# Two split units share one step of exponentials in a fused attention and FFN kernel, with a new order of all work

## The chip, the cores and the metric

The kernel runs on one core of one Trainium2 chip. The metric is the device time of one execution in microseconds; less is better. The core's engines are TensorE (PE; its weight loads are listed as PEld), VectorE (DVE), ScalarE (ACT), GpSimd (POOL) and SyncE (SP), which here issues all DMAs. Each engine works through its own queue in order, and they wait for each other by semaphores.

## The reference

Random-feature attention for 8 batches of 8 heads (576 positions, 64 values a head, 128 features), and an FFN with an exact Gelu over the 4608 resulting rows (512 to 2048 to 512). All is fp32. Cut to what matters:

```python
def phi(x):
    proj = np.einsum('bhsd,md->bhsm', x, omega)
    h = proj - np.sum(x * x, axis=-1, keepdims=True) / 2.0
    h = h - np.max(h, axis=-1, keepdims=True)
    return np.exp(h) / np.sqrt(m)
q_p, k_p = (phi(q_s), phi(k_s))
kv = np.einsum('bhsm,bhsd->bhmd', k_p, v)
z = np.sum(k_p, axis=2)
num = np.einsum('bhsm,bhmd->bhsd', q_p, kv)
den = np.einsum('bhsm,bhm->bhs', q_p, z)[..., None] + 1e-06
attn = (num / den).astype(np.float32)
...
x = np.ascontiguousarray(attn.transpose(0, 2, 1, 3)).reshape(B * S, H * D)
h = x @ w_in
g = 0.5 * h * (1.0 + erf(h * inv_sqrt2))
return (g @ w_out).astype(np.float32)
```

## The kernel before

**Units.** Two heads of one batch are a unit, numbered u = 0 to 31, four to a batch (lines 625 to 640). Units 0 to 7 are computed plainly in fp32 at the start, beside the loading and splitting of the FFN weights. Units 8 to 31 are the split units: fp32 values are taken apart into high and low parts, so that TensorE multiplies narrower numbers and adds the partial products.

**A split unit** runs in three pieces. `split_pre` (line 1069): the transposed k and q come in by DMA, ACT makes the high part (`x_high`, 877, helper line 879), GpSimd the low part (`x_low`, 888); TensorE projects (`proj`, line 896, nine tiles for k; `proj_q`, line 918, four pieces for q); ACT and DVE add the parts and take the maxima; a chain of short steps on ACT and DVE ends in the shifts (`k_shift`, line 914, on GpSimd; `q_shift`, on GpSimd or DVE). `exps_op` (line 1111): one step of ACT, `exps` (line 690), takes exp of the whole buffer, 128x2304, k's half and q's. `split_post` (line 1114): GpSimd rounds exp(k) to fp16 (`k_high`, through the helper line 418), DVE, or GpSimd in the units named by the mask `kl`, makes the low part (`k_low`, line 989); TensorE multiplies with v (`kv_split`, line 1000) and, after a transposition back on DVE and another splitting (`q_back`, `q_high`, `q_low`), makes numerator and denominator (`num`, line 758); ACT and DVE divide (`den` 769, `rcp`, `div` 807), and the result lies in SBUF as the FFN's input.

**The step of exponentials.** ACT holds one table of functions at a time. Exp and Gelu need different ones, and the FFN needs Gelu all along. So `exps` ends, for split units, with a Gelu of one element (line 694) that brings the Gelu table back:

```python
def exps(*us):
    for u in us:
        nc.scalar.activation(u.et, u.et, AF.Exp, bias=kln if u.split else 0.0)
    if us[0].split:
        nc.scalar.activation(wmax[0:1, 1, 0:1], wmax[0:1, 1, 0:1], AF.Gelu)
```

The page shows the two table loads as ACT_TABLE_LOAD of lines 692 and 694.

**Buffers.** The exp buffer exists twice: `et` and `et2` (in the trace `et` and `w`, since `et2` lies in the space of the old weights). `u.eb` (line 634) says which one a unit has: among the split units the second one for even u from 10 on, the first one for the others. So neighbours in the order 10, 11, 12, ... alternate.

**The FFN** runs in 13 blocks of 256 or 384 rows. Block 0 is plain (lines 1182 and 1208), blocks 1 to 3 are split into three partial products (1187; 1211 to 1213), and blocks 4 to 12 form the first matrix product by a scheme of Strassen's kind with seven products (`w_prod`, line 1400, twelve matmuls each), then ACT's Gelu (1425) and high part (1431), DVE's low part (1434), and the second product (`w_mm2`, lines 1498 to 1500: gh x woh, gl x woh, gh x wol). PSUM has eight banks: three for the output sums, two and three for the FFN's first product, its Gelu and the attention.

**The order.** Every piece of work is an `op` with an engine and its dependences, numbered as the program makes it. The string `ORDER` (from line 34) lists all 4950 numbers; `Planner.run` (line 294) emits them in this sequence, letters choosing PSUM banks, and `put` (line 1593) ties each instruction to the one before it on its engine. So each engine's queue is in the string's order. The units are made by the loop around line 1572, which already has a branch for `X['pair']`:

```python
us = [u]
...
    if X['pair'] and u.eb == 1:
        us.append(units[done_u + 1])
    for y in us:
        split_pre(y)
    exps_op(us)
    for y in us:
        split_post(y)
done_u += len(us)
```

Of the kernel before, what the change touches and what calls it, by code (L numbers as in the profile page):

```python
# [28 lines left out]
X = dict(plain=8, kvp=8, eb0=8, ttr=1, pair=0, amax=63, qm=1, xm=0, km=0, prelu=1, n0=4, vs=5,  # L29
# [5 lines left out]
1 2a 3 6 0 7 4 9hda 10 42 11 14f 41 15 12 16 13 44eca 49a 17fh 50 47 51 48 8 22ga 18 45 19 20 43 76 21 46 52bf 23 151 152 157  # L35
77 27ga 55 24 28 53 79ada 56 112 54 31g 154 29c 153 158 57ea 160 62ha 66b 84f 32 58 30 85 111 67 33gc 159 80 82 63 155 86 34
64b 65 35 5 87fh 161 36 114eba 163 81 25 78 115 169 88 83 164 37ca 166 113 59 90 119d 650 92ga 38 165 39 116 40 60 89 91 170
120 68ac 117 93 69 172 167 121 97fa 70 101g 71 175 122dh 171 649 173 123 118 156 685 181 72ae 73 125 126 127ca 74 176 75 177
26 178 652baa 687 102 99e 128 657c 162 651 655 653 98 100 179 187 124 103fg 656 658 104 654 659 132ea 182 136c 183 133 168
105 184 185 106 134h 660ba 663 61 94 107df 108 661 137 664 662 686 95 135 665 129 188 109 138ge 671aa 110 190 139 140 141 193  # L40
666ca 672 667 189 722 688aba 174 96 142hg 292a 191 195 194 675c 199 130 689 196 293 192 180 690 691 294 131 197 296b 146 186
297 198 298 673a 668 295 299 248 669 205 300a 150 721 676 692 674 200 301 147 302 202 249b 306b 201 143 250 203 307 303 251
308 144 677ca 145 252 253 206 693b 207 211 678 256 208 276 679 254 312a 313 304c 680 694 305a 310 695 209 314 757 309 270
318b 212 319 217 213 257 255 148 262 264 425 311 272 316 696ba 214 699 282 697 315 320 317 324a 700 218 698 149 215 322 219
220 321 681ba 204 325 701 326 323 328 329 223 283 682 221 222 683 702ca 224 684 258 225 284 703 330b 707ba 226 327 708 216
# [12 lines left out]
803 1016 555 560a 561 1072 556 1018 390 451 562 789cb 450 1019 559 446 557 447 568b 1077 802 569 1073 1020 1021 965 570 1068
1066 563 566 453 564 790 1022 567 448 565 1078 1023 805 967 791 968 571 1024 574 572 454 575 1025 455 792 582 804 1028 576a
573 577 578 1030 452 969 584b 1032 1051 585 1029 579 586 1031 583 587 590 580 1036 1034 1033 1069ba 1037 1070 1082 1074c 456  # L60
581 1075 591 1079a 1035 970 592a 457 1083 593 1087 1092 1071 1088 971 598 1080 972 588 594 458 1084b 1076 595 1089c 1054 589
599 1085 1093 600b 1156 1096 1081 1097 596 1100 459 601 466 1086 1094aa 597 602 973 1026 1095 1098b 606 608a 1104 1090 609
1052 1101 1099 462 1091 1105 603 1027 1158 607 604 1055 610 1102a 1106b 1038caa 605 1103 1039 611 612 464 1040 1108 1163 1053
1168 614 616b 1041 1107 1159 617 613 1042 618 615 1164 1169 460 1117 1160aa 1109 1165b 1161 1166 1173 1043 624a 465 619 1178
1174 1110 625 806 626 1162 807 461 622 1044 620 1179 1111 1167 1170a 1157 627 1183 621 1045 623 630 632b 1171 467 1112 463
633 628 1172 1113 1184 1175c 1180b 1046 1187 1185aa 634 388 629 1176 1181 635 1047 1191 468 1114 1056 631 638 469 470 1177
391 1195 636 1192 639 1182 1115 1188 637 809a 473 640 1186 477 478 641 810 471 1189b 808 1193c 811 1116 472 479 1196 474 1194
1121 812 1190 1119 1247 815b 1127 1249 816 817 1197a 1048 813 475 1120 1142 1250 1198 1123 1057bc 814 476 1200 1125 642 645
1201 821a 1251aa 1058 1254 1049 643 822 818 827a 480 823 1126 828c 1059 1259 819 1264 1202 1255 1060 1061cb 481 482 1128 1248
820 646 1203 1260 830b 1122 1252 831 1118 1124 1699 483 1062 1063 824 1253 825 832 829b 1701 1064 1145 484 1204 836 833 488  # L70
1129aaa 1130 837 490 1199 1256c 826 1261b 489 834 1143 1269 644 1131 1132 1133 838 1257 1270 835 839a 840 486 1274 1258 485
1262 841 1265 1134 1275 1263 1208 1135 1146 1266b 1271c 491 1278 1267 1136 845 1144 1205 1279 846 1272 1268 1206 487 1276aa
1280b 1282 1700 1137 848b 842 1283 1713 1281 1277 1286 849 1287 850 492 847 1273 854 843 1207 1138 844 1284b 855 1210 493
857a 1050 1285 1147 1212 1288b 1148ca 1149 858 856 1289 1291 1715 1214 859 863 1703 1209 864 1211 1150 1714 1151 1292 494
1716 865 1720 851 852 860 1717ba 1216 853 1725 1233 1152ca 495 1718 1719 800 861 872 1730 1290 1293 862 866b 1217 1139 1294
867 496 868 497 1213 1153 1140 1295 1215 869 873 875a 1296 1220baa 870 1218 1297 1236 1221 874 1222 881 1298 1223 499 876
1726 1721 1219 871 1224 1141 882 1154 1225 877 1303 1155 884b 885 1731 1722c 1727a 498 883 878 1735 1702 1305 1723 1307 1740
890 1309 1705 891 886 1736 1226 1227 879 1728 1741 1306 1704 892 1724 1729 1228 880 1310 1230 1229 1732b 1299 1742aa 1737c
500 1301 1733 1308 893a 1231 1734 894 899 1304 1738 1744 1302 1300 900 887 888 1748 895 1234 1739 1749 1311baa 1312 1313 1314
1315 889 902b 1745 1750c 1743 1746a 1237 1752 1235 1316 901 2249 1317 908 1318 896 897 903 1706 1747 1804 1751 898 1321 1753  # L80
1232 1505 1806 904 905 1238 1322 1811 501 909 1754a 1816 1755 906 503 1324 1817 1239cb 1240 911a 1323 1807 910 1338 1339 912
1340 917 907 913 1808aa 1241 918 919 1506 1341 1242 1342 914 1812 920b 921 1821 1809 1707 915 916 1243bc 1810 1756 1813a 1327
1708 926 1244 922 929a 1805 1822 1325 930 931 1319 1757 1245 923 502 1246 924 1343 1328 1814 925 927 928 1815 935 1758 1818c
1823b 1709 1344 1826 1831 1819 1326 1346 1820 936 1320 1348 932 937 944 938b 1330ac 1824 1759 1329 933 1347 1507 1827 945
1710 939 1835 1711 1760 1331 1832 946 504 1825 940 1828b 1508 941 1349 1712 1532 934 1332 1333 947 1829 948 1839 1761 1350
647 949 1354a 1830 942 1351 1352 1762 1334ba 943 1353 1833ca 1335 1504 1509 950 951 1895 1834 1843 1355 1836 952 1356 953
1360b 1512 1763 1522 1357 1358 1765 1510 1361 1336 1362 1337 954 1359 956 1363 1511 1366a 1844 1840 1847 1845c 1837b 957
# [225 lines left out]
def favor_attention_ffn(ctx: ExitStack, tc: tile.TileContext, qT, kT, v, omT, w_in, w_out, out):  # L313
# [1319 lines left out]
```

## Time and profile before

| | |
|---|---|
| time of three runs, us | 948.91, 952.14, 952.36 (median 952.14) |
| the profiled execution, us | 955.2, its span 953.2 |
| matmuls (instructions on PE) | 7292 |
| busy, us: PE, PEld, DVE, ACT, POOL | 935.6, 669.0, 754.3, 770.6, 480.9 |
| table loads of line 692 and of line 694 | 27 and 24, 1283 ns each |
| Exp of a split unit (line 692) | 24, 2217 ns each |
| mean granted TensorE clock | 0.993 |
| moved by DMA | 71.11 MB, mean 75 GB/s |

A record of a matmul runs from its start to the end of its last result, and neighbours overlap, so PE's busy time is the union of the records. A view by windows gives busy time and count of instructions of each engine in a stretch, then the granted clock, the share of DMA and the rate. In a list by time, the columns are start, duration, engine, line, operation, what it writes and reads, and the count of merged instructions; a bracket names the idle time of the engine ahead of it and who ended it.

### The profile page before, as it was taken

The numbers are of one execution on the slowest core, as the hardware profiler recorded it, in microseconds if no ns is written. First come the engines' busy times: TensorE is split into PE (matmuls) and PEld (weight loads), VectorE is DVE, ScalarE is ACT, GpSimd is POOL, SyncE is SP. The second block draws the span as 40 slices with busy tenths as digits, with TensorE's granted clock in tenths as the row PEclk, the third lists the DMA queues.
The fourth block names the chain that finished last, engine by engine and source line by source line (L and its number), as shares of the span: only waits on it lengthen the run. The fifth ranks groups of instructions, "written<-read, shape, count | busy, mean of one in ns | idle before, by whom it ended". The sixth has DMA issues, their size and how long they took to land.

```text
span 953.2 us, 20399 instructions
## 1 busy us (share of the span) xinstructions
PE 935.6 (98%) x7292; PEld 669.0 (70%) x7292; DVE 754.3 (79%) x2021; ACT 770.6 (81%) x1662; POOL 480.9 (50%) x682
## 2 busy tenths in 40 slices
PE   8999999999999999999999999999999999999998
PEld 7666666666556667777767777777777777777776
DVE  3878999999988899899999899889978775652231
ACT  6988788999789889998899999989688865754453
POOL 1455427788677856575567764863374503140000
PEclk8989999999999999999999999999999999999999
DMA  9864323332322213222212322312112000000000
GB/s 272 242 231 161 114 64 92 87 87 67 75 73 75 66 36 102 64 65 72 76 50 68 87 76 74 89 51 61 39 52 84 2 1 23 2 23 24 1 35 23
DMA packets 46293, 71.11 MB, mean 75 GB/s; under 512 B 13680, under 2 KB 22256, under 8 KB 46192
## 3 DMA queue, kind: packets, MB, share of 16 engines
q1 hardware_dynamic: 46192, 69.81, 25.5%
q8 instruction: 58, 0.95, 0.5%
q14 instruction: 43, 0.35, 0.1%
HBM read 60.36 MB, written 9.44 MB: 73 GB/s over the span
## 4 chain that ended last, share of the span: by engine, by line
PE 57%; ACT 14%; DVE 5%; issue 2%; POOL 1%; DMA 1%; ACTq 0%; DVEq 0%; POOLq 0%
PE p L1400 19%; PE p L1498 7%; PE p L1499 7%; PE p L1500 7%; PE p L1187 5%; PE p L758 2%; PE p L896 2%; PE p L1212 2%; PE p L1211 2%; PE p L1213 2%; PE p L918 2%; PE p L1000 2%; ACT r L879 1%; ACT dt L769 1%; ACT L694 1%
## 5 line engine op out<-in xcount | busy, mean ns | idle before, releaser
L888 POOL TENSOR_TENSOR r<-xt,r 64x256 fp32r<-64x256 f32 (+2 forms) x216 | 168.3, 789 | 166.1 <-ACT r L879 118.9
L1498 PE MATMUL p<-woh,gh 128*128 128x512 f16 (+1 forms) x432 | 161.1, 373 | 0.2 <-ACT o L1220 0.2
L1499 PE MATMUL p<-woh,gl 128*128 128x512 f16 (+1 forms) x432 | 160.3, 371 | 0.4 <-DVE gl L1434 0.4
L1500 PE MATMUL p<-wol,gh 128*128 128x512 f16 (+1 forms) x432 | 160.3, 371 | 0.0
L1400 PEld LDWEIGHTS <-w 128*128 128x128 f16 x1728 | 139.5, 98 | 19.1 <-issue 0.3
L1400 PE MATMUL p<-xh,w 128*128 128x192 f16 (+1 forms) x1152 | 148.2, 243 | 0.0
L1400 PE MATMUL p<-xl,w 128*128 128x192 f16 (+1 forms) x576 | 137.3, 243 | 0.0
L1400 PE MATMUL p<-xh,wih 128*128 128x192 f16 (+1 forms) x432 | 103.3, 243 | 0.0
L1400 PE MATMUL p<-xl,wih 128*128 128x192 f16 (+1 forms) x432 | 103.1, 243 | 0.0
L1400 PE MATMUL p<-xh,wil 128*128 128x192 f16 (+1 forms) x432 | 103.1, 243 | 0.0
L879 ACT CAST r<-xt 128x256 fp32r<-128x256 f32 (+2 forms) x216 | 85.2, 406 | 9.1 <-PE p L896 4.2
L1425 ACT ACTIVATE p<-p,bs 128x384 f32<-128x384 f32 (+1 forms) x108 | 57.9, 539 | 34.6 <-PE p L1400 34.1
L1400 PEld LDWEIGHTS <-wih 128*128 128x128 f16 x864 | 78.5, 98 | 7.6
L1434 DVE SCALAR_TENSOR_TENSOR gl<-p,bs,gh 128x384 f16<-128x384 f32 (+1 forms) x108 | 63.2, 596 | 16.8 <-ACT gh L1431 16.2
L1500 PEld LDWEIGHTS <-gh 128*128 128x128 f16 x432 | 42.3, 98 | 47.1
L1431 ACT ACTIVATE gh<-p,bs 128x384 f16<-128x384 f32 (+1 forms) x108 | 60.9, 570 | 1.1
L1498 PEld LDWEIGHTS <-gh 128*128 128x128 f16 x432 | 42.1, 97 | 28.0
L1187 PE MATMUL p<-xh,wih 128*128 128x384 f16 (+1 forms) x192 | 59.3, 309 | 1.6 <-DVE gl L1203 1.6
L1499 PEld LDWEIGHTS <-gl 128*128 128x128 f16 x432 | 42.4, 98 | 25.1 <-DVE gl L1434 1.2
L1187 PE MATMUL p<-xh,wil 128*128 128x384 f16 (+1 forms) x192 | 59.2, 309 | 0.0
L1187 PE MATMUL p<-xl,wih 128*128 128x384 f16 (+1 forms) x192 | 59.2, 308 | 0.0
L769 ACT ACTIVATE dt<-p,vsc 64x288 f32<-64x288 f32 x96 | 47.6, 496 | 13.8 <-PE p L758 11.7
(236 smaller groups left out, 2590.2 us busy)
## 6 DMA issues: line engine op xcount, KB each, us to landing
xt<-in_kT SPq DMA_DIRECT2D x56, 288.0 KB, 3.9
xt<-in_qT SPq DMA_DIRECT2D x56, 288.0 KB, 3.9
out_x<-o SPq DMA_DIRECT2D x35, 256.0 KB, 2.3
raw<-in_w_in SPq DMA_DIRECT2D x16, 512.0 KB, 5.6
raw<-in_w_out SPq DMA_DIRECT2D x16, 512.0 KB, 4.1
w<-in_v SPq DMA_DIRECT2D x24, 320.0 KB, 4.1
vt<-in_v SPq DMA_DIRECT2D x8, 320.0 KB, 5.6
out_x<-o SPq DMA_DIRECT2D x2, 128.0 KB, 1.7
```

Of the source, the lines that this page charges most:

```text
L758: nc.tensor.matmul(ps[:, 0:HS], a[:, hh], c, start=(i == 0), stop=(i == len(ops) - 1))
L769: nc.scalar.activation(dt[r], ps, AF.Identity, bias=G['vsc', u.b][r, 1:2])
L879: nc.scalar.copy(G['r', u, x][:, 0:b - a], xf[:, a:b])
L888: nc.gpsimd.tensor_tensor(r, xf[D:, a:b], r, op=ALU.subtract)
L1187: nc.tensor.matmul(h[:, 0:t], w, (G['xh', n, j], G['xh', n, j], G['xl', n, j])[k][:, 0:t], start=(i == 0), stop=(i == 3 * NJ - 1))
L1400: nc.tensor.matmul(b[:, g * h:(g + 1) * h], w, x[:, kt], start=first and k == 0, stop=last and k == 6 * GP - 1, skip_group_check=True)
L1425: nc.scalar.activation(h, h, AF.Gelu, scale=G['bs', n][:, 2:3])
L1431: nc.scalar.activation(c_dst('gh', n, q, part), c_in(n, q, part), AF.Copy, scale=G['bs', n][:, 3:4])
L1434: nc.vector.scalar_tensor_tensor(c_dst('gl', n, q, part), c_in(n, q, part), G['bs', n][:, 3:4], c_dst('gh', n, q, part), op0=ALU.mult, op1 ...
L1498: nc.tensor.matmul(acc, gh, woh[:, c, c0:c1], start=begin, stop=False)
L1499: nc.tensor.matmul(acc, gl, woh[:, c, c0:c1], start=False, stop=False)
L1500: nc.tensor.matmul(acc, gh, wol[:, c, c0:c1], start=False, stop=end)
```

## The change

The flag `pair` goes from 0 to 1, and the string `ORDER` is replaced as a whole. With the flag, the loop above takes unit u + 1 along wherever u has the second buffer: u = 10, 12, ..., 30 with 11, 13, ..., 31. Both units' `split_pre` come first, then one `exps` over both buffers (Exp, Exp, one Gelu), then both `split_post`. Units 8 and 9 keep steps of their own. The program then has 4939 numbers instead of 4950, eleven steps of ACT fewer, and as many steps as before on every other engine. The mask `kl` stays as it was: of units 8 to 31, numbers 9, 13, 17, 21, 25 and 29 have k's low part made by GpSimd. The diff, cut to its core:

```diff
-X = dict(plain=8, kvp=8, eb0=8, ttr=1, pair=0, amax=63, qm=1, xm=0, km=0, prelu=1, n0=4, vs=5,
+X = dict(plain=8, kvp=8, eb0=8, ttr=1, pair=1, amax=63, qm=1, xm=0, km=0, prelu=1, n0=4, vs=5,
          tx=4, ss=4, xh=8, gh=3, xp=0, qs=1431655680, kl=572662272, wl=21845, wg=0, px=0)
...
 ORDER = """
-1 2a 3 6 0 7 4 9hda 10 42 11 14f 41 15 12 16 13 44eca 49a 17fh 50 47 51 48 8 22ga 18 45 19 20 43 76 21 46 52bf 23 151 152 157
-77 27ga 55 24 28 53 79ada 56 112 54 31g 154 29c 153 158 57ea 160 62ha 66b 84f 32 58 30 85 111 67 33gc 159 80 82 63 155 86 34
...
+6 1 0 7 42 4 2b 9haa 3 10 12 14e 41 151 15 11 44bca 47 16 49d 17eg 8 50 13 51 48 18 43 45 20 152 153 76 154 52da 157 46 19
+22fa 57ha 21 53 27ea 55 31c 79bga 77 23 56 54 58 32 158 29d 82 155 84c 28 30 111 159 160 62aa 33fe 161 85 114dha 163 86 63 34
...
```

## Rows read from the trace of the kernel before

**Rows 1.** The page: busy us (share of the span) x instructions of each engine

```profile
PE 935.6 (98%) x7292; PEld 669.0 (70%) x7292; DVE 754.3 (79%) x2021; ACT 770.6 (81%) x1662; POOL 480.9 (50%) x682
```

**Rows 2.** Windows, by stage: PE, PEld, DVE, ACT, POOL, then clock, DMA share, GB/s

```profile
0.00:75.00 75.00, 67.50 (x503) 51.29 (x504) 51.95 (x132) 58.79 (x140) 33.10 (x29) 0.91 0.83 252
75.00:200.00 125.00, 122.78 (x761) 82.23 (x760) 114.68 (x270) 106.03 (x213) 69.21 (x90) 1.00 0.33 94
200.00:350.00 150.00, 149.21 (x948) 92.02 (x947) 135.62 (x390) 132.04 (x295) 110.31 (x159) 1.00 0.26 70
350.00:600.00 250.00, 247.13 (x2058) 184.96 (x2056) 230.78 (x676) 232.99 (x511) 154.77 (x231) 1.00 0.27 73
600.00:850.00 250.00, 249.09 (x2081) 184.46 (x2079) 192.62 (x499) 196.86 (x411) 111.55 (x171) 1.00 0.13 36
850.00:953.20 103.20, 99.89 (x953) 74.05 (x950) 28.60 (x58) 43.84 (x97) 1.99 (x4) 1.00 0.07 24
```

**Rows 3.** List by time, PE, two places between 400 and 496 us

```profile
400.53 0.53 PE L1000 MATMUL p<-vb,vt 128*128 128x129 f16 x8 [0.16 <-DVE w L807]
400.90 0.33 PE L1400 MATMUL p<-xh,w 128*128 128x192 f16 x2
...
490.11 0.25 PE L1400 MATMUL p<-xh,wih 128*128 128x192 f16 x1
...
491.10 0.38 PE L1498 MATMUL p<-woh,gh 128*128 128x512 f16 x1
...
494.12 0.38 PE L1500 MATMUL p<-wol,gh 128*128 128x512 f16 x1
...
495.13 0.39 PE L1498 MATMUL p<-woh,gh 128*128 128x512 f16 x1
```

**Rows 4.** Windows, 400 to 600 us: L1400, L1498, L896, L918, L758, L1000, then everything

```profile
400.00:600.00 200.00, 84.01 (x904) 74.56 (x905) 1.00 0.26 72
400.00:600.00 200.00, 48.85 (x128) 12.44 (x128) 1.00 0.26 72
400.00:600.00 200.00, 17.60 (x73) 11.53 (x73) 1.00 0.26 72
400.00:600.00 200.00, 15.07 (x62) 9.92 (x62) 1.00 0.26 72
400.00:600.00 200.00, 14.83 (x84) 12.04 (x84) 1.00 0.26 72
400.00:600.00 200.00, 9.67 (x144) 7.40 (x144) 1.00 0.26 72
400.00:600.00 200.00, 197.36 (x1653) 147.84 (x1652) 184.20 (x540) 186.33 (x411) 126.33 (x184) 1.00 0.26 72
```

**Rows 5.** List by time, ACT: unit 10's step of exponentials

```profile
217.81 1.28 ACT L692 ACT_TABLE_LOAD   x1
219.11 2.22 ACT L692 ACTIVATE w<-w,kln 128x2304 f32<-128x2304 f32 x1
221.35 1.28 ACT L694 ACT_TABLE_LOAD   x1
222.64 0.20 ACT L694 ACTIVATE wmax<-wmax 1x1 f32<-1x1 f32 x1
```

**Rows 6.** Groups of ACT by line: table loads, busy us, mean ns, idle before

```profile
L692 ACT ACT_TABLE_LOAD x27 | 34.6, 1283 | 0.5
L694 ACT ACT_TABLE_LOAD x24 | 30.8, 1283 | 0.4
```

**Rows 7.** List by time, ACT and PE: a step, the next stall

```profile
491.12 1.28 ACT L692 ACT_TABLE_LOAD   x1
...
500.89 0.73 PE L896 MATMUL p<-om,r 128*128 128x256 f32 x4 [0.71 <-DVE xsb L807]
```

**Rows 8.** Windows: the two stretches of the lower clock level

```profile
18.70:25.60 6.90, 6.90 (x38) 5.75 (x38) 2.19 (x6) 5.00 (x13) 2.58 (x2) 0.51 0.79 213
52.90:59.75 6.85, 6.85 (x40) 6.19 (x40) 3.44 (x11) 6.83 (x13) 2.58 (x2) 0.50 0.55 183
```

More of the change, by code (lines that the diff above doesn't have):

```diff
@@ L37 @@
[L37 to L45, printed above, removed]
@@ L84 @@
[L84 to L87, printed above, removed]
-1841a 1364 1367 1372a 1764 1518 1897 1373c 1365 1368 1369 1838 1846 1374b 1381 1382 1766 1769 1902 1375b 2250 1767 1842 1770
@@ new lines @@
+2449 1640 2079 1641 1642 2365 2367 2073 2369 2366 1620 1625 2445aa 1618 2446 2368 2371 1643 1626 1621 1644 2373 1619 2447
+1629 2375baa 2370 2372 2083 2450a 2376 2458 2377 2378 2374 1622 1627 2379 1628 1668 2404 2451 2080 2455c 2452 2459 2460a 2463
+1499 2464 1645b 1630 1623 2380 2468 2412 2388 2381 2406 2472 2456 2382 2963 1624 1669 2457 2469 1670 2391 1631 2461 1632
+2465b 2473 2470ca 2466 2405 2462 2471 1671 2492 1672 2476 2467 2474a 2480 1673 2477 2481 2402 2494 1647e 1646a 2475 2403
+2478b 2086 2385 2499 2482a 2389 2392 2504 1649 1648 2408 2483 2409 2495 2479 1651 1674 2407 2500 2383 2410 1650 2493 2411
@@ new lines @@
+2386 1675 2485 2496aa 2497 2501b 2413 1655 2486 2487 2384 2502 2498 1652 2088 2503 2414aaa 2415 2505 2416 2417 1653 2506b
+2390 2507 2087 2418 2509 1660 1676 2419 1654 2420 2514 1661 1656 2510 2421 2508 2393 2488 1662 1663 2489 2427 1677 2394ba
+2395 1678 2519 2520 1664 2396 1679 2100a 2544 2515 1680 1657 1665 2084 2521ca 2397 2511b 1658 2424 2512 1659 2090 2085 2522
+1666 1681 1502 2081 2965 2523 1682 2092 1683 2513 2516c 2430 2524 2517 1667 2398ab 2089 2490 1684 1685 2527 1688 2091 2975
+2518 2399 2400 2484 2531 2094 1689 2096 2525c 2401 2532 1686 2428 1690 2093 1691 2101b 2526 2102d 2104 1692 2103 1687 2106
@@ new lines @@
+2095 2977 2528 2529a 2098 2097 2107 2105 2533c 2982 2110 2099 2964 2422 2987 2431 1694 2530 2111 2108 2534 1695 2112 2978
+1696 2536 2109 2535 2113 2537 2115 2119 2491 2116 2123c 2114 2538 2125b 2539 2120 2146a 2540 2541 2387 2121 2122 2542 2966
+2988 2147 2117 2983 2126 2124a 2976 2543 2127 2128 2118 2129 2546 2429 2148b 2133 2149 2150 2130 2425 2432 2552 2134 2548
+2151 2152c 2545 2153 2423 2569 2547 2553 2131 2554 2549 2550 2979ca 2556baa 2555 2551 2138 2557 2572 2587 2980 2558 2559 2560
+2154 2132 2155 2585 2561 2562 2981 2563 2589 2992 2984b 2989c 2985 2593 2586 2990 2590 2967 2591 2997 3002 2986 2592 2142
@@ new lines @@
+2636 2223 3075 2201 2616 2974 2204 2617 3168 2209 3069 2631 2224 3164 2632 2205 3078 3510 2212 2637 2210 2629 2202 2618ba
+2633 2225 3159 2213 2794 3076 2226 2638 2640 2619 3169 2227 2206 3157 2211 2620 2228 2214 2229 2207 2215 3077 2648a 2649b
+2230 3080 2231 2232 2621 3079 2650c 2233 2639 2236 2651 2641 3084 2237 3511 3103 3086 3081 2238 3160ca 3082 3173 2239 3161
+3085 2652 3088 2642 3087 3083 3165b 3162 3089 3090caa 3091 2643 2644 3174 3119 3178 3166 2653 3167 3104 3092 3093 3179 2645
+3094 2654 3095 2646 3170b 2658 2234 3096 3171 3105 3097 3175c 3183 3172 2663 2655 2647 3127 2659 3121 3180b 3120 3125 3176
@@ new lines @@
+2656 3177 3184 3187 3106 3181 3122 3191 2242 3185ca 3182 2664 3188 3207 3195 3192 3186 2657 2667 3189b 2243 3098 3107 3190
+3196 3209 3123 2668 3210 3193c 2660 3197b 3214 3219 2235 3194 2671b 3198 2665 2661 2694a 3211ba 3215 2240 3212 3128 3216c
+3124 3217 2695 2666 3208 3100 3224 3142 3220 3218 3221a 3126 2669 3213 2662 3229 2670 3117 3225 3222 3108 3200 2672a 2244
+2673e 2696c 2697 3226b 3223 3234 2698 3201 3227 3202 3118 3230 3228 3231a 3235 3232 3233 3203 3523 3238 3099 2675 3242 3101
+3243 3236ba 3246 3204 2677 3244a 3237 3239 3145 2795 3245 2674 2678 3129baa 3247 2679 3130 2801 2699 3131 2700b 3240a 3132
@@ new lines @@
+4627b 4617 4611 4622 4628d 4619 4624 4630 4629 4632 4211 4621 4214 4215 4216 4633 4634 4631 4623 4636 4217 4625 4637 4641
+4642 4638 4645 4220 4212 4643 4649e 4646 4635 4221 4650b 4639 4647 4640 4213 4651c 4672a 4673 4218 4674b 4653 4779 4644 4652
+4675 4648 4655 4219 4654 4659 4664 4676 4660 4656 4665 4222 4668 4657 4684d 4658 4677 4669 4661 4775 4678c 4679 4776 4680
+4681 4685a 4686b 4682 4687 4777 4688 4666 4690 4689 4694 4683 4662 4691 4699 4707 4692 4708 4695 4703 4667 4663 4693 4670
+4671 4709 4700 4710 4719c 4720a 4780 4711 4712 4713 4721e 4714 4701 4715 4722 4716 4723 4781 4717 4696 4718 4742 4697 4724
@@ L233 @@
+4857 4858 4850 4856 4861 4829 4837 4859 4830 4866 4838 4767 4862 4867 4874 4875 4876 4834 4877 4878 4870 4879 4860 4880 4871
+4863 4881 4882 4883 4886e 4888c 4887a 4890 4884 4889 4892 4885 4909 4910 4891 4893 4864 4865 4896 4872 4894 4901 4873 4911
+4897 4912 4902 4913 4898 4914 4915 4916 4868 4869 4917 4903 4771 4905 4918 4919 4895 4920 4921 4906 4899 4900 4907 4922 4908
+4923 4924 4904 4927 4925 4928 4929 4930 4931 4932 4933 4936 4934 4926 4935 4937 4938
 """
```

340 lines of the change are left out of this document (161 added, 179 removed), and 3 rows, old and new, of the table ORDER.

## The prediction

> **What bounds the kernel now.** I read the page's busy times first: TensorE is busy for 935.6 us of a 953.2 us span, ACT for 770.6, DVE for 754.3 [rows 1]. Then the same by stage, since a mean over stages hides which limit holds where [rows 2]. There the reader should see three things. TensorE's idle time is 7.5 us in the first 75 us (75.00 less 67.50) and 2.2 us up to 200 us; from 200 to 850 us, the stretch in which nearly all the changed work runs, it is only 0.8 + 2.9 + 0.9 = 4.6 us; after 850 us it is 3.3 us. Second, between 200 and 600 us DVE and ACT are nearly full as well (135.6 and 132.0 of 150, then 230.8 and 233.0 of 250), and after that they thin out. Third, the first 75 us have a DMA share of 0.83 and a granted clock of 0.91.
>
> A busy TensorE could still be an idle one in disguise: a record of a 128x512 matmul lasts 0.38 us while the next starts after 0.21 us [rows 3], so a wait shorter than the overhang doesn't show as idle. I therefore worked out what the stretch from 400 to 600 us needs if every matmul starts as soon as one of its kind can. Spacings [rows 3]: twelve 128x192 matmuls from 490.11 to 491.10 us, 82.5 ns each; fourteen 128x512 from 491.10 to 494.12 us, 0.216 us each; the six of line 758 from 494.12 + 0.216 to 495.13 us, 0.132 us each; eight of line 1000 from 400.53 to 400.90 us, 0.046 us each. Counts [rows 4]: 904 of L1400; 128 of L1498 and as many of L1499 and L1500, which line 1498's function issues with it; 73, 62 and 84 of the attention's L896, L918 and L758, all taken at L758's spacing; 144 of L1000. That is 74.6 + 82.9 + 28.9 + 6.6 = 193.0 us of 200, where the records show 197.4 busy. So the stretch loses about 7.0 us, 2.7 times the 2.6 us of idle shown. Scaled by 2.7, the 4.6 us between 200 and 850 us become **12 us: all that any change outside the first 200 us can win without taking matmuls away**. TensorE's clock is at its upper level (2.4 GHz) there, granted 1.00 [rows 2].
>
> **The change, part by part.** TensorE's work: nothing is removed or added, 0 us. The flag makes the units with the second buffer for exp (u = 10, 12, ..., 30) take the next unit into their step, so 24 steps of the split units become 13.
>
> *The step of exponentials.* One now is: table load 1.28, Exp over 128x2304 2.22, table load 1.28, a Gelu of one element 0.20; from 217.81 to 222.84 us, 5.03 us of ACT [rows 5]. A shared one keeps both Exp and one pair of loads: 1.28 + 2.22 + 2.22 + 1.28 + 0.20 with the gaps of these rows is 7.25 us. Each pair thus saves 2 x 5.03 - 7.25 = 2.81 us, and eleven pairs (24 steps counted by their second table load [rows 6]) take **31 us off ACT**. None of it is on TensorE's own sum: it pays only where TensorE waits for ACT. Of the 12 us lost, if all were owed to these steps, 11/24 would return, 5.5 us; at the other end, nothing does. The nearest rows are the stall at 500.89 us, which follows a step that began at 491.12 us [rows 7]: there a backlog of ACT and DVE reaches TensorE. DVE, as full as ACT, isn't relieved, so I take the half, -2.6 us.
>
> The Trainium skill (ScalarE: Activation LUTs, What ACT_TABLE_LOAD costs) puts each switch at about 1.28 us of load and 1.38 us of drain. This case's rows show the load at 1.28 us and the Exp starting 0.02 us after it, with no drain; by the page ACT would be relieved of 22 x 2.66 = 58.5 us, by the rows of 31, and either meets the same ceiling on TensorE.
>
> *The longer block.* Whatever waits for ACT behind a shared step (Gelu and splitting of the FFN, evacuation of PSUM) waits 7.25 us instead of 5.03, eleven times. TensorE lives on ready work meanwhile. Rows 7 bound how much: the step began at 491.12 us and TensorE first sat idle before 500.89 - 0.71 = 500.18 us, so it had about 9 us. 7.25 us is inside this, with 1.8 us to spare. Bounds: 0, and 2.2 us (7.25 - 5.03) for each of eleven, 24 us. The stall of these rows, after a block of 5.03 us, is 0.71 us, and most steps have none; nearest to that I take +1 us for all eleven.
>
> *The added wait.* The second Exp stands behind the first in ACT's queue and waits for its own unit's shifts on GpSimd or DVE; behind it are the FFN's Gelus, and TensorE's accumulations wait for these. Read along the new order, with spacings as above, TensorE's work between the last projection of the second unit and the shared step is 12.9 us in the median and 7.9 us at least (before: 20.9 and 9.9). I take 0 us: that cover is TensorE's own work, and where it is gone each late microsecond costs one.
>
> *Both buffers.* The first unit's post-processing follows closer: TensorE's work from the step to its first k-v product is 7.2 us in the median (3.2 at the least, units 10), before 13.8. Its Exp ends 3.50 us into the step, so 3.7 us remain for the high and low parts on GpSimd and DVE. The second unit has 25.8 us. The next pair's projections come only as the first unit's buffer is read out, in lockstep; inside the +1 above.
>
> *Loads on other queues, and GpSimd's low parts:* the mask kl is unchanged, so that part of the title is 0; DMAs are the same in number, and after 200 us their share is 0.27 or less [rows 2]. They are moved no further past another queue than the steps they feed.
>
> *The order anew.* The first 200 us are searched again too, though nothing in them is changed. There 9.7 us are idle and two stretches of 6.9 us run at the lower clock level (granted 0.51 and 0.50 [rows 8], both before 60 us), each costing 3.4 us. A new order can win or lose such a stretch or shift the idle, but the DMA share there is that of the weights, which both orders load. I take 0, with -3.4 and +3.4 for the range. Counted along TensorE's work, the first product of each FFN block and the attention's last one stand within 5 us of where they stood.
>
> **Sum.** The profiled execution took 955.2 us, 2.0 more than its span; the runs' median is 952.1, 3.1 less. 955.2 + 0 - 2.6 + 1 + 0 = 953.6 for a profiled one, and the same -1.6 on the median gives **950.5 us**. About 0.5%, 4.8 us, is what a measurement of this kernel can tell from no change: 947.4 to 956.9 counts as the same.
>
> **Rivals.**
> *B, the relief shows.* ACT's backlog is what TensorE's lost time comes from, and all of 5.5 us returns (946.6), perhaps with one slow-clock stretch less (943.2). For it: the stall behind a step at 491 us [rows 7]; ACT at 93% from 350 to 600 us [rows 2]. Against: DVE at 92% beside it. I put it at 945; chance 0.26.
>
> *C, the shared step starves TensorE.* Place: the eleven shared steps, from about 230 to 820 us. ACT is away for 7.25 us, no FFN bank is evacuated, and the first unit's k-v product and the next pair's projections come in a burst on a DVE that has no slack. Price: the stall of 0.71 us, which followed a 5.03 us block, plus half of the 2.2 us more, 1.8 us a step: 11 x 1.8 = 20 us if all do, 10 if half do. It decides from the point where TensorE's ready work, 9 us at 491 us, falls under 7.25. For it: the shorter distances in the new order. Against: TensorE idles for 0.9 us in all from 600 to 850 us, where ACT has slack (196.9 of 250), so half of the pairs should be safe. 952.1 + 10 = 962; chance 0.20.
>
> *D, TensorE's busy time is hollow and ACT is the bound.* Then 31 us come off: 921. The Trainium skill (Perfetto Trace Analysis, Identifying the Most-Contended Engine) warns that matmul busy time is a poor measure of the distance to the roof, as matmuls are pipelined. The rows bear it out in kind and not in size: 197.4 us of records hold 193.0 us of need. Chance 0.02.
>
> *E, the loads don't go*, if a table load still stood between the two Exp: ACT as before, the time 952. No row of before shows two such Exp in a line; but it is the Gelu of line 694 that calls the other table, and it now comes once a pair. Chance 0.02.
>
> **How the numbers follow.** Forecast (little moves, 947.4 to 956.9) 0.50, B 0.26, C 0.20, D 0.02, E 0.02. Faster by over 0.5%: B and D, 0.28. Same: the forecast and E, 0.52. Slower: C, 0.20. Range: down to 943.2 (B with a clock stretch) and up to 960, which takes in the milder half of C (8 us lost); about 0.05 is left below and 0.12 above.
>
> **What would show it.** Right: lines 692 and 694 show 16 and 13 table loads (27 and 24 before [rows 6]); ACT's busy time some 740 us; TensorE's unchanged at 7292 matmuls, idle from 200 to 850 us between 2 and 7 us. Rival B: that idle near 1 us and the 128x512 rows without stalls behind a step. Rival C: stalls of TensorE of 1 us and more some 5 to 10 us after each second table load, released by gl, gh or an xt row. The forecast is wrong if the first 75 us move by more than 3.4 us, since I can't price the new order there from these rows.

## The result, and the profile after

| | before | after |
|---|---|---|
| the three runs the prediction started from, us (median) | 952.14 | |
| sixteen runs of each, us (median; lowest to highest) | 948.83 (947.91 to 959.27) | 954.75 (951.56 to 958.79) |
| ratio after to before, with its 95% interval | | **1.0055 [1.0038, 1.0071]** |
| profiled execution, us (its span) | 955.2 (953.2) | 953.45 (951.2) |

The change costs 0.55%, some 5 us. Executions in the slow state are left out of the ratios, here and below (one, of 1364.26 us at a mean granted clock of 0.653, in the kernel with the steps undone); nor is a ratio quite the quotient of the two medians. 954.75 lies inside the range given, but the forecast was that little moves, with 1.6 us won, and the change loses some 5 us, just over the 0.5% at which the prediction drew the line. In the code behind `ORDER` the lines of after are one lower than before's (L691 for L692); in the kernels of the experiments they are off by up to six.

First the page of after: its busy times (they answer to [rows 1]) and, from its groups of ACT by line, the table loads ([rows 6]).

```profile
PE 933.2 (98%) x7292; PEld 666.2 (70%) x7292; DVE 753.5 (79%) x2021; ACT 743.3 (78%) x1629; POOL 487.2 (51%) x682
...
L691 ACT ACT_TABLE_LOAD x16 | 20.5, 1283 | 0.3
L693 ACT ACT_TABLE_LOAD x13 | 16.7, 1283 | 0.2
```

ACT is 27.3 us less busy, with 33 instructions and 22 table loads fewer: the relief is there, though 27.3 us and not the 31 of the forecast. TensorE has the same 7292 matmuls. A shared step, in the list by time of after, ACT (it answers to [rows 5]; start, duration, operation):

```profile
433.46 1.28 ACT L691 ACT_TABLE_LOAD   x1
434.76 2.22 ACT L691 ACTIVATE w<-w,kln 128x2304 f32<-128x2304 f32 x1
436.88 2.21 ACT L691 ACTIVATE et<-et,kln 128x2304 f32<-128x2304 f32 x1
439.10 1.28 ACT L693 ACT_TABLE_LOAD   x1
440.40 0.20 ACT L693 ACTIVATE wmax<-wmax 1x1 f32<-1x1 f32 x1
```

The step takes 7.14 us, and nothing stands between the two Exp. The windows by stage, of after ([rows 2]): length, then PE, PEld, DVE, ACT and POOL busy, the granted clock, DMA share, GB/s.

```profile
0.00:75.00 75.00, 66.42 (x522) 49.29 (x523) 50.26 (x132) 60.92 (x146) 33.97 (x30) 0.95 0.82 247
75.00:200.00 125.00, 124.68 (x767) 83.82 (x767) 114.72 (x287) 107.66 (x220) 78.29 (x98) 1.00 0.37 105
200.00:350.00 150.00, 149.75 (x974) 93.62 (x971) 137.43 (x387) 126.99 (x285) 107.37 (x156) 1.00 0.23 64
350.00:600.00 250.00, 244.51 (x2015) 181.90 (x2014) 229.44 (x649) 217.52 (x482) 157.47 (x229) 1.00 0.26 70
600.00:850.00 250.00, 249.94 (x2096) 185.55 (x2094) 195.81 (x516) 188.57 (x409) 109.19 (x169) 1.00 0.14 40
```

TensorE's idle time from 200 to 850 us was 4.6 us and is 5.8: 0.25 + 5.49 + 0.06. It has nearly gone from two stages and grown in the middle one, though ACT lost 15.5 us of work just there (232.99 to 217.52). Two windows of 25 us show where. First after, then before in a second trace of it (the first experiment below):

```profile
425.00:450.00 25.00, 22.56 (x190) 16.27 (x188) 22.53 (x62) 21.05 (x41) 15.16 (x22) 1.00 0.15 38
450.00:475.00 25.00, 23.66 (x194) 17.75 (x192) 23.81 (x76) 18.31 (x49) 12.87 (x16) 1.00 0.38 106
```

```profile
425.00:450.00 25.00, 25.00 (x207) 18.37 (x206) 23.33 (x69) 21.86 (x47) 12.17 (x15) 1.00 0.33 89
450.00:475.00 25.00, 24.95 (x227) 20.16 (x226) 23.40 (x79) 20.20 (x55) 15.41 (x26) 1.00 0.18 51
```

Most of the idle time (2.44 + 1.34 = 3.8 us of the 5.5) is around one of the eleven shared steps, that of units 18 and 19 (it is the one printed above, from 433.46 us). The stalls there, from the list by time of after, PE; the bracket names the idle time and who ended it:

```profile
428.06 0.26 PE L1399 MATMUL p<-xh,wih 128*128 128x192 f16 x1 [0.55 <-DVE wih L1412]
...
433.50 0.33 PE L1399 MATMUL p<-xh,w 128*128 128x192 f16 x2 [1.00 <-ACT p L1409]
...
446.93 0.50 PE L917 MATMUL p<-r,om 128*128 128x288 f32 x2 [0.36 <-ACT lo L899]
...
447.95 0.50 PE L917 MATMUL p<-r,om 128*128 128x288 f32 x2 [0.52 <-DVE nm L905]
...
451.64 0.50 PE L917 MATMUL p<-r,om 128*128 128x288 f32 x2 [0.16 <-POOL r L887]
...
460.69 0.70 PE L999 MATMUL p<-vb,vt 128*128 128x129 f16 x12 [0.41 <-DVE xsb L806]
```

The block of ACT itself (433.46 to 440.60) is covered: TensorE is busy for 7.10 of its 7.14 us. It stalls ahead of the block, while unit 19's last steps go through DVE and ACT, and behind it, where the next pair's q projections (L917) come and wait for ACT, DVE and GpSimd in turn.

**A finer measure.** Idle time hides waits shorter than the time by which one record overlaps the next. So for every matmul I took the time from its start to the next start, less the usual spacing of its kind in the second trace of before (the first experiment). I summed this loss by place; the place is the sum of usual spacings so far, some 15 us less than the time in the execution. The loss in groups of places, in us:

```
kernel                     0-150  150-175  175-400  400-450  450-700  700 on   sum
before (second trace)        5.2      2.5      4.9      0.8      9.3     0.4   23.1
after                        8.4      0.6      4.5      5.3      7.8     0.8   27.4
start_before_rest_after      7.7      1.3      4.5      5.4      7.9     0.8   27.6
start_after_rest_before      8.0      0.5      4.9      0.8      9.4     0.3   23.9
before_no_tables             5.4      2.5      5.4      0.8      7.3     0.4   21.8
before_small_vmax            8.4      0.5      4.6      0.8      9.3     0.3   23.9
after_small_vmax             8.0      0.6      4.7      4.8      7.8     0.8   26.7
after_three_moved            7.7      0.6      4.5      5.4      7.9     0.8   26.9
before_start_changed         6.9      0.5      4.4      0.8      9.3     0.4   22.3
before_two_pairs             9.0      2.5      4.6      0.8     10.8     0.3   28.0
before_pair_18               8.1      2.5      4.3     21.2      9.4     0.4   45.9
after_unpaired              10.9      0.6     20.3      7.5     28.2     3.2   70.7
```

After against before: +3.2 in the start, -1.9 at 150, +4.5 around units 18 and 19, -1.5 in all the rest; sum +4.3, where the spans differ by 4.6 (951.2 and 946.6). The group 0 to 150 holds the stretches at the lower clock, and these differ from one execution to the next.

### The profile page after: what moved, and what is told of

It reads as the page before. It is cut to its first block, busy times and chain, and to the rows that moved or that the text cites. A ratio compares the mean times of both kernels' runs of the same rounds, so it can differ in the third digit from the quotient of the medians.

```text
span 951.2 us, 20400 instructions
## 1 busy us (share of the span) xinstructions
PE 933.2 (98%) x7292; PEld 666.2 (70%) x7292; DVE 753.5 (79%) x2021; ACT 743.3 (78%) x1629; POOL 487.2 (51%) x682
## 5 line engine op out<-in xcount | busy, mean ns | idle before, releaser
L887 POOL TENSOR_TENSOR r<-xt,r 64x288 fp32r<-64x288 f32 (+2 forms) x216 | 173.3, 813 | 130.5 <-ACT r L878 101.2
L1498 PE MATMUL p<-woh,gl 128*128 128x512 f16 (+1 forms) x432 | 160.3, 371 | 0.0
L1498 PEld LDWEIGHTS <-gl 128*128 128x128 f16 x432 | 42.4, 98 | 24.4 <-DVE gl L1433 0.2
```

The costliest lines, as they stand in the source:

```text
L887: nc.gpsimd.tensor_tensor(r, xf[D:, a:b], r, op=ALU.subtract)
L1498: nc.tensor.matmul(acc, gl, woh[:, c, c0:c1], start=False, stop=False)
```

## The experiments

**The kernel before once more**, unchanged, for the scatter and a trace without a lower-clock stretch.

> The kernel before once more, unchanged, for a second profile and as a measure of scatter. By every theory the ratio is 1.000, within 0.002. Between executions the mean granted clock should fall into steps (0.998, 0.996, 0.993), one for each stretch of about 6.8 us at the lower level, and each step should cost about 3.4 us of span; if the clock isn't what separates executions, spans at one clock differ as much as those between clocks.

Measured: 948.65 us, ratio 0.9989 [0.9977, 1.0001]. Its clock over the places of [rows 8], and over the stretch of after that has the lower clock, as windows of the second trace of before and of after:

```profile
18.70:25.60 6.90, 6.45 (x72) 4.91 (x70) 5.06 (x12) 6.87 (x19) 4.11 (x3) 1.00 1.06 295
52.90:59.75 6.85, 6.77 (x39) 5.21 (x36) 6.29 (x15) 6.82 (x13) 4.40 (x4) 1.00 0.85 306
```

```profile
50.20:57.10 6.90, 6.90 (x41) 6.20 (x41) 4.69 (x12) 5.61 (x10) 3.46 (x4) 0.51 0.62 202
```

So the two stretches of [rows 8] belong to that execution and not to the kernel. Over 25 executions of before beside this run, the 14 whose mean clock was 0.998 or more took 948.1 to 950.4 us and the 11 at 0.996 and less took 950.4 to 954.1. By their times, two of the prediction's three runs were of the second sort: its 952.14 stood some 3 us too high.

**Start and rest apart.** Only `ORDER` is spliced: the first 160 us come from one order, the rest from the other, and the flag `pair` is that of the rest. The diff, cut, of the second of the two kernels against before:

```diff
 ORDER = """
-1 2a 3 6 0 7 4 9hda 10 42 11 14f 41 15 12 16 13 44eca
+6 1 0 7 42 4 2b 9haa 3 10 12 14e 41 151 15 11 44bca
...
```

> The order of the changed kernel, but its first 707 steps (some 160 us, up to the first split unit's step) are those of the kernel before, in that order; all after them is the changed kernel's, shared steps included. Theory S (the start: the new order of the first 160 us brings a stretch at the lower clock level into most executions): ratio to before 0.998 to 1.002, mean clock mostly 0.998. Theory R (the rest: the shared steps or the new order behind 160 us make TensorE wait): 1.004 to 1.007. Both by half: 1.002 to 1.004.

> The mirror image: the first 710 steps from the changed kernel, the rest from the kernel before, one step of exponentials for each unit. Theory S: ratio to before 1.003 to 1.007, mean clock mostly 0.996 or less. Theory R: 0.998 to 1.002. Both by half: 1.002 to 1.004.

Measured: before's start with after's rest 1.0042 [1.0023, 1.0060]; after's start with before's rest 1.0014 [1.0000, 1.0027]. They add up to the whole, 1.0055: about 4.0 us of the loss belong to the part with the shared steps (the table has 3.2 behind 175 us), 1.3 to the new start. The loss around units 18 and 19 goes with the rest of the order: 5.4 us in the group 400 to 450 with after's rest, 0.8 with before's.

**The shared step undone in the new order.** At each of the eleven places stand two steps again, one right behind the other; nothing else is moved. The flag:

```diff
-X = dict(plain=8, kvp=8, eb0=8, ttr=1, pair=1, amax=63, ...
+X = dict(plain=8, kvp=8, eb0=8, ttr=1, pair=0, amax=63, ...
```

> The changed kernel with the flag back at 0 and nothing else moved: at the place of each shared step stand two steps one behind the other, each with its own pair of table loads and its own Gelu, so ACT has eleven blocks of 10.06 us instead of 7.25 and 31 us more work. Theory C (the length of ACT's block makes TensorE wait): slower than the changed kernel by 11 x 1 to 2.8 us, ratio to before 1.017 to 1.038. Theory N (ACT's load and its blocks don't reach TensorE): within 0.2% of the changed kernel, ratio 1.004 to 1.007.

Measured: 993.78 us, 1.0463 [1.0441, 1.0486], some 39 us more than after and above the 1.038 that theory C allowed. TensorE, from the list by time of this kernel, behind the double step of units 12 and 13 (ACT away from 288.98 to 299.05):

```profile
301.88 1.28 PE L891 MATMUL p<-om,r 128*128 128x256 f32 x4 [2.69 <-DVE nm L901]
302.96 0.54 PE L1182 MATMUL p<-xh,wih 128*128 128x384 f16 x1
303.29 0.53 PE L1182 MATMUL p<-xh,wil 128*128 128x384 f16 x1
...
305.38 0.33 PE L1182 MATMUL p<-xl,wih 128*128 128x384 f16 x1
305.54 0.33 PE L1182 MATMUL p<-xh,wih 128*128 128x384 f16 x1
```

ACT is away for 10.07 us in place of 7.14, and TensorE stands still for 2.69 of the 2.9 us more. At nine of the eleven places, this one among them, it is 2.6 to 3.5 us; at units 18 and 19 it is 1.0 and 1.96, and at the last pair nothing over 1 us. Behind seven of these nine stalls the granted clock drops as well, which adds to the ratio: here the spacing is 0.32 us up to 304.9 us and then 0.165. Behind the other two (354.95 and 763.56 us) it stays at 1.00. So rival C's mechanism is real, and its threshold lies between 7.14 and 10.07 us at these places: the new order holds work for TensorE ready for the block that it has, and hardly any more.

**Relief of ACT and of DVE by themselves.** In either kernel the split units' Exp became a Copy that writes 1.0. The table loads go with it (48 in before, 26 in after), and so do the units' exponentials. In two other kernels the maximum over v reads one of ten tiles.

```diff
-            nc.scalar.activation(u.et, u.et, AF.Exp, bias=kln if u.split else 0.0)
+            if u.split:
+                nc.scalar.activation(u.et, u.et, AF.Copy, scale=0.0, bias=1.0)
...
```

```diff
-        nc.vector.tensor_reduce(vmax[:, u.k:u.k + 1], u.v[:, :, 0:D], ...
+        nc.vector.tensor_reduce(vmax[:, u.k:u.k + 1], u.v[:, 0:1, 0:D], ...
```

> The kernel before, in its own order, with a Copy that writes 1.0 in place of Exp in the split units (so what these units compute is not the reference): no table change is left there, ACT loses 48 loads of 1.28 us, 61 us of work, and its blocks fall from 5.03 to about 2.4 us. Theory A (ACT's backlog behind the steps is what TensorE waits for, so relief of ACT pays): 5 to 9 us faster, ratio 0.990 to 0.995. Theory D (relief of ACT doesn't pay, since DVE and GpSimd, as full as ACT, hold TensorE up): within 2 us, ratio 0.998 to 1.000.

> The same cut in the changed kernel (Copy of 1.0 for Exp in the split units, which then don't compute the reference): 26 loads less, 33 us of ACT, and shared blocks of about 4.6 us in place of 7.25. Theory A: the 17 us that TensorE loses behind 200 us shrink to under 11, ratio to before 0.996 to 0.999. Theory D: 0 to 2 us less than the changed kernel, ratio 1.003 to 1.006. If shortening the block by 2.6 us gives nothing while lengthening it by 2.8 cost 39 us, the order's ready work on TensorE covers just the block that it was made for.

> The kernel before with the maximum over v (line 1024, DVE, 0.81 us, 24 times) taken over one of ten tiles instead of all; the rest of the maximum is left out. DVE has some 16 us less to do, nothing else changes. Theory D (DVE is what TensorE waits for): 3 to 6 us faster, ratio 0.993 to 0.997. Theory A: within 1.5 us, ratio 0.998 to 1.001.

> The same cut in the changed kernel: the maximum over v taken over one of ten tiles, 16 us of DVE less. Theory D: the losses ahead of the shared step at 433 us go, 3 to 6 us less than the changed kernel, ratio to before 0.999 to 1.003. Theory A: as the changed kernel, 1.004 to 1.007.

Measured, in this order: 0.9998 [0.9981, 1.0015], 1.0025 [1.0009, 1.0040], 0.9972 [0.9959, 0.9986], 1.0031 [1.0015, 1.0046]. The page's busy times without tables, of before and of after:

```profile
PE 929.1 (98%) x7292; PEld 664.5 (70%) x7292; DVE 756.1 (80%) x2021; ACT 706.4 (75%) x1614; POOL 487.5 (52%) x682
PE 935.3 (98%) x7292; PEld 669.7 (70%) x7292; DVE 753.8 (79%) x2021; ACT 707.5 (74%) x1603; POOL 488.2 (51%) x682
```

In before, over twice the change's relief (64 us off ACT) doesn't move the time: in the table, 450 to 700 gains 2.0 us and 175 to 400 loses 0.5. In the changed kernel 36 us off ACT bring about 3 us. DVE's 13 us (754.1 to 740.8) bring 0.3% in before; in the table this is one stall near 165 us (2.5 to 0.5 in the group 150 to 175). The loss around units 18 and 19 stays through all of it. With DVE relieved it is 4.8 us in the changed kernel. With the tables gone it is as large as in after, within 0.1 us by the same count, though ACT's block there takes 4.2 us (436.37 to 440.59) in place of 7.14. So neither the length of this block nor DVE's maxima are its cause.

**Splices in the middle.** After's order for one stretch in before, or the reverse, with the shared steps that lie in it.

> The kernel before, but in the stretch from about 320 to 575 us the work stands in the changed kernel's order, with the five shared steps of units 14 to 23; ahead of it and behind it the order of before, one step a unit. Theory M (the loss sits in this stretch, at few of its steps): ratio to before 1.003 to 1.006. Theory E (every shared step costs its 0.4 us, eleven of them 4.2 us): 5 x 0.4 = 2 us, ratio 1.001 to 1.003.

> The reverse, with the start of before as well: the first 160 us and the stretch from about 320 to 590 us in the order of before with one step a unit, the rest in the changed kernel's order, with five shared steps (units 10 to 13 and 26 to 31). Theory M: ratio to before 0.997 to 1.000, since the changed kernel's trace loses 1.7 us less outside that stretch. Theory E: 2 us, ratio 1.001 to 1.003.

> The kernel before, with the changed kernel's order from about 395 to 485 us alone, which holds one shared step, that of units 18 and 19 (at 433 us of the changed kernel, where its trace loses 4.2 us within 12 us ahead and 20 behind). Theory M: 2 to 4 us, ratio 1.002 to 1.004. Theory E: 0.4 us, 0.999 to 1.001.

> The kernel before, with the changed kernel's order from about 470 to 575 us alone: the two shared steps of units 20 to 23, in place of four steps around which before's own trace loses 4 to 6 us. Theory M: little is lost here, ratio 0.998 to 1.001. Theory E: 0.8 us, 1.000 to 1.002.

Measured, in this order: 1.0136 [1.0117, 1.0155], 1.0060 [1.0044, 1.0076], 1.0066 [1.0052, 1.0081] and 1.0100 [1.0082, 1.0119]. All four lie above what the theory under test allowed, and as ratios they say little: the spacing shows 3 to 6 us lost near six of the nine seams, in part at the lower clock. That the two orders aren't at the same point of their work there is the likely reason, but it wasn't tested. What stays clean is the group 400 to 450: 5.4 and 5.3 us in the two kernels with after's order there, 0.8 in the other two. The loss belongs to the order of that stretch with its shared step, and needs nothing of the order ahead of it.

**Is DVE's queue the cause there?** Three of DVE's steps ahead of the shared step, a low part xl and two maxima over v, moved behind a later sum (L1412):

```diff
-2095 2977 2528 2529a 2098 2097 2107 2105 2533c 2982 2110 2099 2964 2422 2987 2431 1694 2530 2111 2108
+2095 2977 2528 2529a 2098 2097 2107 2105 2533c 2982 2110 2422 2987 2431 1694 2530 2111 2099 2108
...
```

> The changed kernel with three steps of DVE moved behind a following sum of FFN block 5 (L1412): the low part xl of one piece, and the maxima over v of units 21 and 22 (L1023). Nothing else is moved. In the changed kernel TensorE loses 5.3 us by spacing in the bins 400 to 450 of its own work, around the shared step of units 18 and 19, against 0.8 us in the kernel before; the first stalls there wait for just these sums. If it is DVE's queue that is crowded ahead of the shared step, the first bin's 2.2 us fall to about 1 us, and the second's 3.1 us by up to 1 us; the ratio moves by no more than 0.002 (1.003 to 1.005). If it is the block of the shared step itself that TensorE feels there, whatever stands in DVE's queue, both bins keep their 2.2 and 3.1 us.

Measured: 1.0059 [1.0046, 1.0073], and 2.2 and 3.2 us of loss at the places 400 to 425 and 425 to 450 (2.2 and 3.1 in after): nothing gained. What PE waits for, from 410 to 475 us in this kernel (us, times, longest):

```profile
PE p L1394 <- ACT p L1404: 0.9, 1, 0.9
...
PE p L1394 <- DVE xl L1363: 0.4, 1, 0.4
```

The stall of 0.55 us for the sum is gone, and in its place TensorE waits 0.4 us for the xl that was put behind it. The wait was passed on, and the theory that these three steps are the cause falls.

**The step shared in the old order.** Before's own order, the flag limited to some units; only the steps that the new dependences force aside are moved.

```diff
-    if X['pair'] and u.eb == 1:
+    if X['pair'] >> u.k & 1 and u.eb == 1:
```

> The kernel before with only two of the eleven shared steps, units 22 and 23 and units 26 and 27, and its own order kept: 51 of some 4950 steps had to give way to the new dependences, all else stands as before. Theory: sharing a step costs because the two units' work before and after it has to be made in lockstep, and an order that was not made for it pays for that. It expects 2 us and more for each of the two (stalls of TensorE near both), ratio 1.004 or above. Rival: sharing is free by itself and only the new order around units 18 and 19 was unlucky; it expects 0.999 to 1.001 and no more loss than before at the two places.

> The kernel before with one shared step only, that of units 18 and 19, at the place of unit 19's own step, and its own order kept: 76 steps stand more than 1.5 us elsewhere along TensorE's work, all of them between 406 and 436 us of it. If sharing costs at this place whatever the order, because ACT and DVE are full there and the two units' work crowds behind one step (as around units 22 and 23, where it cost 1.3 us, and not at 26 and 27, where it cost 0.2), the bins 400 and 425 rise from 0.2 and 0.6 us to 4 us and more together, ratio 1.003 to 1.005. If the 4.5 us were a flaw of the new order alone, they stay under 1.5 us together, ratio 0.999 to 1.0015.

Measured: units 22/23 and 26/27 shared, 1.0006 [0.9991, 1.0021]; units 18/19 alone, **1.0193 [1.0175, 1.0211]**. The two pairs cost less than the 2 us each that the theory wanted, the single one far more than the 1.005 expected. One thing that sets the three apart is how far from each other their two steps stood in the old order. The Exp of these pairs, from the list by time of before's second trace, ACT:

```profile
415.84 2.22 ACT L692 ACTIVATE w<-w,kln 128x2304 f32<-128x2304 f32 x1
...
447.82 2.22 ACT L692 ACTIVATE et<-et,kln 128x2304 f32<-128x2304 f32 x1
...
528.33 2.22 ACT L692 ACTIVATE w<-w,kln 128x2304 f32<-128x2304 f32 x1
...
536.56 2.22 ACT L692 ACTIVATE et<-et,kln 128x2304 f32<-128x2304 f32 x1
```

Units 18 and 19 stood 32.0 us apart, 22 and 23 8.2 us, 26 and 27 6.4 us (637.6 and 644.0). The two near pairs cost 1.3 us and 0.2; the first is mostly a single stall, from the list of that kernel, PE:

```profile
546.61 0.48 PE L890 MATMUL p<-om,r 128*128 128x256 f32 x2 [1.03 <-DVE nm L900]
```

Sharing 18 and 19, from the list by time of that kernel, first ACT, then PE:

```profile
446.48 1.28 ACT L686 ACT_TABLE_LOAD   x1
447.78 2.21 ACT L686 ACTIVATE w<-w,kln 128x2304 f32<-128x2304 f32 x1
449.90 2.20 ACT L686 ACTIVATE et<-et,kln 128x2304 f32<-128x2304 f32 x1
452.10 1.28 ACT L688 ACT_TABLE_LOAD   x1
453.39 0.20 ACT L688 ACTIVATE wmax<-wmax 1x1 f32<-1x1 f32 x1
453.50 0.39 ACT L873 CAST r<-xt 128x256 fp32r<-128x256 f32 x1
```

```profile
446.03 0.59 PE L890 MATMUL p<-om,r 128*128 128x256 f32 x2
454.85 0.77 PE L890 MATMUL p<-om,r 128*128 128x256 f32 x2 [8.23 <-POOL r L882]
456.91 0.76 PE L890 MATMUL p<-om,r 128*128 128x256 f32 x2 [1.30 <-DVE nm L900]
458.82 1.79 PE L994 MATMUL p<-vb,vt 128*128 128x129 f16 x18 [1.14 <-DVE nm L900]
462.37 0.76 PE L890 MATMUL p<-om,r 128*128 128x256 f32 x2 [1.76 <-ACT kvz L1009]
```

Unit 20's projections (L890) are what TensorE has next. They need ACT's high part (L873), which stands behind the shared step, then GpSimd's low part, and their sums go into the buffer that unit 18 holds until its exp is read out. In the old order unit 18's step lay 32 us ahead of unit 19's; now all of this hangs on one block, and TensorE is out of work 0.1 us after ACT has left. Of the 20 us lost some are the lower clock that follows; the window behind the stall, of the same kernel:

```profile
455.00:475.00 20.00, 13.86 (x67) 9.02 (x68) 10.41 (x36) 5.88 (x16) 6.15 (x11) 0.58 0.34 89
```

So sharing has a price at this place in the old order too, where little was rearranged for it, and the searched order pays less, 4.5 us. That distance alone sets the price isn't shown: units 14 and 15 (30.9 us), 24 and 25 (29.3), 28 and 29 (31.7) and 30 and 31 (60.1) stood as far apart or farther in the second trace of before, and in after no 25 us around their places lose over 0.3 us more than in before, by the count of the table. So an order can make room for such a pair. Why the searched one didn't for units 18 and 19, and how much of the 4.5 us another could take away, wasn't tried beyond the three moved steps and stays open.

**The new start alone, in the old order:** before's order, with after's from some 85 to 160 us, no step shared.

> The kernel before with the order of one stretch only replaced: TensorE's own work from 70 to 140 us (some 85 to 160 us of the execution) in the changed kernel's order, all the rest, the first 70 us among it, as before. No step is shared. The changed kernel's order of this stretch shows 2 us less loss of TensorE behind it (0.6 against 2.5 us in the bin at 150), while its first 70 us seem to bring one stretch more at the lower clock. If these two are independent, this kernel takes about 2 us less than the one before: ratio 0.998, clock as the one before. If the lower-clock stretches hang on the order behind 70 us too, the ratio is 1.000 to 1.002 and clocks of 0.996 and less are common.

Measured: 948.12 us, 0.9995 [0.9980, 1.0011], 9 of 12 executions at a clock of 0.998 or more. This stretch keeps the gain of the new start (the group 150 to 175 falls from 2.5 to 0.5 us). The more frequent lower clock goes with after's first 70 us, which are left out here: with all of after's start and before's rest, none of 12 executions reached 0.998. Of the kernels that leave no work out it has the shortest trace (span 945.9 against 946.6), by an amount that the times can't tell from nothing. The stall that it takes away, in the second trace of before:

```profile
163.88 0.27 PE L1187 MATMUL p<-xh,wih 128*128 128x256 f16 x1 [1.57 <-DVE gl L1203]
```

## Why the prediction was right or wrong

**The edits were read rightly.** There are 16 and 13 table loads, ACT at 743.3 us, a step of 7.14 us (7.25 forecast), no load between the two Exp, 7292 matmuls: rival E is out. TensorE is the bound, as read from the spacing: rival D is out, since 64 us off ACT gave 0.9998. The forecast was -2.6 + 1 + 0 = -1.6 us. The traces have -1.5 in all the rest, where ACT's relief would show, +4.5 around units 18 and 19 and +1.3 in the start, 4.3 us.

**The step that failed first is the -2.6 us for ACT's relief**, with rival B behind it. It shared out TensorE's lost 12 us between ACT and DVE because both are over 90% busy from 350 to 600 us. That an engine is busy doesn't make it what TensorE waits for: with 64 us off ACT in the old order TensorE's loss behind 175 us falls by only 1.5 us, and the time not measurably. The term should have been 0 to -1.5. The lone stall of [rows 7], on which the half rested, ended on a step of DVE, as its row says.

**The second is the +1 us for the longer block and the lockstep.** The traces give 4.5 us, all at one place. Three errors lie in it. I bounded TensorE's ready work by one place, 9 us at 491 us, and took it for all eleven; at unit 19's step the old order has 0.1 us of it as soon as the steps are shared. Nor were there 9 us without ACT at that place, for ACT was back long before TensorE's stall, so the row shows no more than 5 us covered (trace of before, ACT):

```profile
496.17 1.02 ACT L769 ACTIVATE dt<-p,vsc 64x288 f32<-64x288 f32 x2
```

And I set the price by the length of the block (2.2 us more), not by what sharing moves: unit 18's step, its reading out and the next pair's projections by up to 32 us. The prediction even named the lockstep, that the next pair's projections come only as the first unit's buffer is read out, and filed it as "inside the +1 above" without a price of its own. In the old order this costs 20 us at units 18 and 19, and the trace shows how; that the same makes up the 4.5 us of the new order is argued, not shown.

**Rival C had the mechanism and missed the shape.** It named starvation behind the shared steps, expected it evenly, 1.8 us at five or eleven of them, and gave 962. In after ten of eleven places cost next to nothing and one paid 4.5 us, on both sides of the block. That there is a threshold is confirmed: a block 2.9 us longer costs 2.6 to 3.5 us at nine places.

**The start, taken as 0 with ±3.4, is +1.3 us** (1.0014): 1.9 us won at 165 us, and about one lower-clock stretch of 3.4 us more in many executions. Of after's sixteen executions three reached a clock of 0.998. The bound was right, the middle was off by 1.3.

**The base was 3 us high.** The median of three times was taken as the kernel's time, and the profile that held two lower-clock stretches [rows 8] as its normal execution. Had the sum been made on 948.8, -1.6 would have given 947.2, and the miss would have been larger. The band that counts as the same, 947.4 to 956.9, would have ended at 953.6 (948.8 + 4.8): that 954.75 lies in it is luck with the base. The wider range, moved down by the same 3.3 us, would have ended at 956.7 and still held it.

**The idle from 200 to 850 us**, 5.8 us, lies within the 2 to 7 that the forecast gave as its sign. That sign couldn't tell a small loss from none.

**On the price of a switch**, the rows of after show a load of 1.28 us and nothing behind it: Exp starts 0.02 us after the load of 433.46, and 22 loads fewer took 27.3 us off ACT's busy time. The Trainium skill (ScalarE: Activation LUTs, What ACT_TABLE_LOAD costs) adds 1.38 us of drain to each load. No row here shows that drain; an estimate with that page's 2.66 us a switch, 22 x 2.66, would have been 58.5 us. For the time of this kernel either figure was without weight.

## What to carry to other kernels

Work taken off an engine that isn't the bound is worth what the bound's own waits on it are, and one kernel that leaves that work out prices it: here it was nothing in the kernel before and some 3 us in the changed one. When two units' steps are merged, list for every pair how far apart they stood, since everything tied to the earlier step moves with it, and the bound engine must have other work for that time. In the three pairs tried in the old order the price rose with that distance; in the searched order four pairs as far apart cost next to nothing, so the distance says where to look and not what will be paid. And before forecasting half a percent, see whether the executions shown differ among themselves by a stretch at the lower clock.

## What the runs showed of the hardware

The scatter of this kernel comes in steps. In the profiles a stretch of 6.9 us at 0.51 of the clock costs 3.4 us, and the times follow: among the 25 executions, before took about 949 us at a mean clock of 0.999 and 1.000, about 952 at 0.996, and 952 to 954 at 0.993 to 0.995. In the profiles of before and after the stretches come in the first 75 us, where TensorE is idle for 7 to 9 us, and how often depends on the order of the work there: 14 of 25 executions of before had a mean clock of 0.998 or more, 3 of 16 of after, and none of 12 with after's start and before's rest.

A stall of TensorE in the middle can be followed by one too. In the kernel with the steps undone a wait of 2.69 us was followed by some 3 us at half the rate (granted clock 0.77 from 302 to 309 us), and in the one with units 18 and 19 shared the window behind the 8.23 us has a clock of 0.58 over 20 us. There a microsecond of waiting cost more than a microsecond. It isn't so behind every stall: after 2.64 us of waiting at 354.95 us, in the first of these kernels, the granted clock stayed at 1.00.
